# One load queue in order of use, split PSUM banks and quarter-width first matmuls in the opening of a grouped-query attention kernel

## Chip, cores, metric

The kernel runs on one core of one Trainium2 chip. The metric is the device time of one execution in microseconds (us). The time is 1.7 to 2 us longer than the span of the profile, which runs from the first to the last recorded event. All runs quoted here are fast (full granted clock), so they may be compared. "Faster" and "slower" mean by over 2%; the gain predicted here, 0.8 us, is about a tenth of that.

## The reference, cut to what matters

Two independent problems A and B of the same shapes; their outputs are concatenated.

```python
# x: 16 x 32 x 1024 (512 tokens of 1024), wq: 1024 x 4096, wo: 4096 x 1024, all bf16
# caches: 16 x 4 x 512 x 128; 32 query heads of 128 on 4 key heads
q = (x @ wq).reshape(B, Sq, 32, 128)            # projection, 32 heads
scores = q @ k.T * 128 ** -0.5                   # per head
o = softmax(scores) @ v
out = o.reshape(B, Sq, 4096) @ wo
```

## The kernel before

TensorE (PE) needs x transposed, with the 1024 features on the partitions. Four x tiles of 128 tokens (256 KB each; x0 to x3 below) are loaded into SBUF, the on-chip memory, and transposed on PE into PSUM, the memory in banks that PE writes to; VectorE (DVE) and ScalarE (ACT) copy the result back to SBUF. Then the first two heads are projected, in two halves of 256 tokens, while the rest is still loading. From head 2 on, a stream of matmuls of 512 columns keeps PE busy to the end. The change touches only what comes ahead of head 2. In the code, `warm_up(n)` does n matmuls on zeros that nobody reads, so that PE is busy before its data comes; the two between the transposes and the heads are called the filler below. In the profiles, PEld is PE's loading of weights, and SP (SyncE) and ACT each issue loads on a queue of their own.

```python
for j in range(2):                                   # loads: SP's queue and ACT's queue in turn
    for e, eng in enumerate((nc.sync, nc.scalar)):
        tt = 2 * j + e
        eng.dma_start(out=x_sb[:, tt, :], in_=x_v[:, tt, :])
    for e, eng in enumerate((nc.sync, nc.scalar)):   # heads 2j, 2j+1: lower and upper features
        cs, ns = slice(e * HC, (e + 1) * HC), slice(2 * j * DH, 2 * (j + 1) * DH)
        eng.dma_start(out=wq_tiles[0, 0][:, cs, ns], in_=wq_v[:, cs, ns])
load_wq(0, 1)                                        # 1 MB, SP; then keys, values, weights ...
# ... cut ...
def transpose_x(tt):
    xT_ps = psum.tile([P, DC, P], BF16, name="xT_ps", tag="s")
    for dc in range(DC):
        nc.tensor.transpose(xT_ps[:, dc, :], x_sb[:, tt, dc * P:(dc + 1) * P], ident[:])
    ts = slice(tt * P, (tt + 1) * P)
    nc.vector.tensor_copy(out=xT[0][:, 0:HC, ts], in_=xT_ps[:, 0:HC, :])
    nc.scalar.copy(out=xT[0][:, HC:DC, ts], in_=xT_ps[:, HC:DC, :])
# ... cut: first_heads(h, half) does 8 matmuls of 256 columns into head h's bank ...
warm_up(8)          # matmuls on zeros, nobody reads them
transpose_x(0)
transpose_x(1)
warm_up(2)
first_heads(0, 0)
transpose_x(2)
transpose_x(3)
first_heads(1, 0)
first_heads(0, 1)
first_heads(1, 1)
```

## Time and profile before

| | before |
|---|---|
| time at the prediction, median of 3 (range) | 350.65 us (350.25 to 350.69) |
| span of the profiled execution | 349.1 us (its time: 350.9 us) |
| PE busy | 340.7 us, 98% |
| first transpose starts | 4.90 us |
| head 2 starts / its copy starts | 11.54 / 13.70 us |

The page's busy times (busy us, share of the span, instructions) and the chain that ended last, by engine and by line:

```profile
PE 340.7 (98%) x2163; PEld 221.0 (63%) x2204; DVE 283.4 (81%) x421; ACT 179.6 (51%) x196; POOL 8.9 (3%) x21
...
PE 94%; DMA 3%; issue 1%; DVE 1%; ACT 0%; SPq 0%
```

PE bounds the kernel. The DMA share of the chain (11.7 us) lies wholly in the opening. The start of the same chain in order of time (start, us, what):

```profile
0.86 4.00 DMA x_sb<-in_A_x_dram
4.85 0.02 issue
4.87 7.71 DMA wq_sb<-in_A_wq_dram
12.58 0.05 issue
12.63 10.32 PE q_ps L312 x47
```

So the kernel waited for x tile 0 until 4.85, and then for a weight load that was issued at 4.87 and landed at 12.58. It is issued so late because it is the ninth load to be issued (the 1 MB load, written after it, goes ahead of it on SP's queue): the loads share eight semaphores, and the ninth waits until the first, x tile 0, has landed and its semaphore is free. The timeline of the opening (start, us of the whole group, engine, line, operation; in brackets the idle time of the engine ahead of it and what ended it):

```profile
4.90 1.24 PE L493 MATMUL xT_ps<-ident,x_sb 128*128 128x128 bf16 x16
5.73 0.87 DVE L497 COPY xT<-xT_ps 128x512 bf16<-128x512 bf16 x2 [3.28 <-PE xT_ps L493]
...
6.19 1.07 ACT L498 COPY xT<-xT_ps 128x512 bf16<-128x512 bf16 x2 [4.08 <-DVE xT L497]
...
6.66 1.26 PE L507 MATMUL q_ps<-xT,wq_sb 128*128 128x256 bf16 x8
...
7.92 1.07 PE L493 MATMUL xT_ps<-ident,x_sb 128*128 128x128 bf16 x16
...
8.82 2.81 PE L507 MATMUL q_ps<-xT,wq_sb 128*128 128x256 bf16 x24
...
11.54 11.40 PE L312 MATMUL q_ps<-xT,wq_sb 128*128 128x512 bf16 x50
...
13.70 0.58 ACT L320 CAST qT<-q_ps 128x512 bf16<-128x512 f32 x1 [3.59 <-PE q_ps L312]
...
15.43 0.58 ACT L320 CAST qT<-q_ps 128x512 bf16<-128x512 f32 x1 [1.14 <-PE q_ps L312]
```

Two things are to be read here. ACT's first copy was released by DVE's copy, not by PE: both read one PSUM bank, and DVE goes first. The Trainium skill, "PSUM — Partial Sum Buffer", section "PSUM bank collisions raise a hardware error", says that two engines may not access one bank and quadrant at once, reads included; the kernel's order agrees (DVE's first copy ends at about 6.16, ACT's starts at 6.19). And head 2's copy at 13.70 is a mark: the copies that follow it come every 1.73 us.

The windows view of the stretch in which four pieces of 256 KB landed (the last of x0 and x1 at 4.85, the last of the next four at 7.87; last columns: DMA share, that is the times of all packets over the time of 16 engines, which comes out above 1 here, and GB/s of all traffic):

```profile
core 0: us, PE busy (x) PEld busy (x) DVE busy (x) ACT busy (x) POOL busy (x), PEclk, DMA share, GB/s
4.85:7.87 3.02, 2.86 (x27) 1.95 (x26) 0.85 (x2) 1.07 (x2) 0.00 (x0) 1.00 1.11 344
```

### The profile page before, as it was taken

Reading aid. Unit: us, or ns where it says so; the run is one execution under the profiler, and the core shown is the slowest. Engines: PE = TensorE matmul, PEld = TensorE weight load, DVE = VectorE, ACT = ScalarE, POOL = GpSimd, SP = SyncE. Lnnn points to the kernel's source line nnn. Section 1 sums busy time; section 2 is a strip of 40 time slices with the busy share of each in tenths; the row PEclk is TensorE's granted clock in tenths of the full one; section 3 lists DMA queues with packets and bytes.
Section 4 is the critical chain, followed back from the end, with each engine's and each line's share of the span. In section 5 each row is a group of like instructions: output and inputs, shape, how many; then the busy total and the mean of one; then the engine's idle time right before and its main releaser. Section 6 shows DMA issues by size and latency. Waiting matters only on the chain.

```text
span 349.1 us, 5460 instructions
## 1 busy us (share of the span) xinstructions
PE 340.7 (98%) x2163; PEld 221.0 (63%) x2204; DVE 283.4 (81%) x421; ACT 179.6 (51%) x196; POOL 8.9 (3%) x21
## 2 busy tenths in 40 slices
PE   8999999999999999999999999999999999999995
PEld 4556666666666666666666666666666666666554
DVE  2218888988988898898889999999989999899710
ACT  2247667666666666666654454454454445445000
POOL 0000000000000000000000000000000000000010
PEclk9999999999999999999999999999999999999999
DMA  7999999999996999999999659996579975400000
GB/s 242 275 251 339 181 274 264 254 269 249 270 214 176 199 233 233 296 275 210 305 313 192 175 126 289 348 199 122 135 258 287 284 182 97 116 17 0 15 32 20
DMA packets 125085, 71.70 MB, mean 205 GB/s; under 512 B 73632, under 2 KB 124064, under 8 KB 125056
## 3 DMA queue, kind: packets, MB, share of 16 engines
q1 hardware_dynamic: 122848, 68.24, 81.1%
q0 software_dynamic: 720, 1.97, 1.6%
q10 hardware_dynamic: 1488, 1.11, 1.1%
q8 instruction: 18, 0.29, 0.4%
q14 instruction: 11, 0.09, 0.1%
HBM read 51.38 MB, written 2.10 MB: 153 GB/s over the span
## 4 chain that ended last, share of the span: by engine, by line
PE 94%; DMA 3%; issue 1%; DVE 1%; ACT 0%; SPq 0%
PE f_ps L331 31%; PE q_ps L312 30%; PE ob L431 16%; PE s_ps L371 16%; DMA wq_sb<-in_A_wq_dram 2%; DMA x_sb<-in_A_x_dram 1%; DVE parts L390 0%; PE sums L407 0%; DVE o_sb L343 0%; ACT o_sb L341 0%; DVE cs L399 0%; PE ok_ps L614 0%; SPq L651 0%
## 5 line engine op out<-in xcount | busy, mean ns | idle before, releaser
L379 ACT ACTIVATE p_sb<-s_ps,shift 128x1024 bf16<-128x1024 f32 x128 | 142.5, 1114 | 113.1 <-PE s_ps L371 100.4
L390 DVE TRANSPOSE_TENSOR_REDUCE parts<-p_sb 128x32 f32<-128x1024 bf16 x128 | 158.2, 1236 | 21.5 <-ACT p_sb L379 20.9
L331 PE MATMUL f_ps<-wo_sb,oT 128*128 128x512 bf16 (+1 forms) x524 | 127.9, 367 | 0.4
L312 PE MATMUL q_ps<-xT,wq_sb 128*128 128x512 bf16 x475 | 124.8, 380 | 0.6
L371 PE MATMUL s_ps<-qT,kT 128*128 128x256 bf16 x512 | 76.8, 273 | 0.9
L431 PE MATMUL ob<-p_sb,v_sb 128*128 128x256 bf16 x512 | 76.8, 273 | 0.6
L331 PEld LDWEIGHTS <-oT 128*128 128x128 bf16 x544 | 53.0, 98 | 33.8
L312 PEld LDWEIGHTS <-wq_sb 128*128 128x128 bf16 x496 | 48.3, 98 | 35.1 <-DMA wq_sb<-in_A_wq_dram 0.6
L371 PEld LDWEIGHTS <-kT 128*128 128x128 bf16 x512 | 56.9, 113 | 20.9
L431 PEld LDWEIGHTS <-v_sb 128*128 128x128 bf16 x512 | 50.1, 98 | 19.8 <-DVE oT L453 0.3
L453 DVE TENSOR_TENSOR oT<-r,ob 128x512 bf16<-128x512 f32 x64 | 43.9, 685 | 12.7 <-PE ob L431 9.3
L320 ACT CAST qT<-q_ps 128x512 bf16<-128x512 f32 x62 | 36.1, 583 | 23.7 <-PE q_ps L312 20.8
L418 DVE STREAM_TRANSPOSE r<-rall 128x512 f32<-128x512 f32 x64 | 45.5, 711 | 2.2
L407 PE MATMUL sums<-cs,fold 128*128 128x16 f32 x64 | 22.9, 357 | 0.1
L343 DVE CAST o_sb<-f_ps 128x512 bf16<-128x512 f32 (+1 forms) x16 | 10.8, 673 | 10.8 <-PE f_ps L331 10.0
L399 DVE TENSOR_REDUCE cs<-parts 128x16 fp32r<-128x64 f32 x64 | 16.9, 264 | 2.2
L407 PEld LDWEIGHTS sums<-cs,fold 128*128 128x128 f32 x64 | 12.1, 190 | 8.3 <-DVE cs L399 0.9
L345 POOL DMA_DIRECT2D out_dram<-o_sb x15 | 8.2, 549 | 329.7 <-DVE o_sb L343 299.0
L416 DVE RECIPROCAL rall<-sums 128x16 f32<-128x16 f32 x64 | 14.1, 220 | 0.0
L341 ACT CAST o_sb<-f_ps 128x256 bf16<-128x256 f32 x1 | 0.4, 372 | 22.1 <-PE f_ps L331 22.1
L497 DVE COPY xT<-xT_ps 128x512 bf16<-128x512 bf16 x4 | 1.7, 424 | 5.3 <-PE xT_ps L493 5.3
L484 PE MATMUL warm_ps<-warm 128*128 128x512 bf16 x10 | 4.2, 580 | 1.3 <-DVE warm L230 1.3
(26 smaller groups left out, 22.8 us busy)
## 6 DMA issues: line engine op xcount, KB each, us to landing
v_sb<-in_A_v_cache_dram SPq DMA_DIRECT2D x16, 512.0 KB, 4.9
wq_sb<-in_B_wq_dram SPq DMA_DIRECT2D x8, 1024.0 KB, 6.5
wo_sb<-in_A_wo_dram SPq DMA_DIRECT2D x8, 1024.0 KB, 7.6
v_sb<-in_B_v_cache_dram SPq DMA_DIRECT2D x16, 512.0 KB, 4.2
wo_sb<-in_B_wo_dram SPq DMA_DIRECT2D x8, 1024.0 KB, 9.2
wq_sb<-in_A_wq_dram SPq DMA_DIRECT2D x7, 1024.0 KB, 8.0
out_dram<-o_sb POOLq DMA_DIRECT2D x15, 128.0 KB, 3.1
kT<-in_A_k_cache_dram SPq DMA_TRANSPOSE x64, 4.5
```

The source lines that it names most:

```text
L312: nc.tensor.matmul(ps[:], lhsT=w[:, dc, (h % 4) * DH:(h % 4 + 1) * DH], rhs=xT[pr][:, dc, :], start=(dc == 0), stop=(dc == DC - 1),)
L320: nc.scalar.copy(out=qT[pr, g][:, :, hl, :], in_=ps[:].rearrange("p (b s) -> p b s", s=SQ),)
L331: nc.tensor.matmul(ps[:, 0:width], lhsT=oT[pr, tt][:, h, :], rhs=wo_tiles[pr, nh, h // REP][:, h % REP, off:off + width], start=(h == 0), ...
L371: nc.tensor.matmul(s_ps[:, c, :], lhsT=kT[:, i % GRP, c, :], rhs=qT[pr, g][:, b, :, :].rearrange("p h s -> p (h s)"), start=True, stop=True,)
L379: nc.scalar.activation(out=p_sb[:], in_=s_ps[:], func=ACTF.Exp, bias=shift[:], scale=SCALE)
L390: nc.vector.tensor_reduce(out=parts[j][:, q, :, :].rearrange("p c h -> p (c h)"), in_=st[i]["p"][:].rearrange("p c (h s) -> p (c h) s", s=SQ),
L399: nc.vector.tensor_reduce(out=cs[:], in_=parts.pop(j)[:].rearrange("p q c h -> p q h c"), axis=AX.X, op=ALU.add,)
L407: nc.tensor.matmul(sums[:], lhsT=fold[:].rearrange("p r s -> p (r s)"), rhs=cs[:].rearrange("p q h -> p (q h)"), start=True, stop=True,)
L416: nc.vector.reciprocal(out=rall[:, j, :], in_=pair.pop(j)[:])
L418: nc.vector.transpose(out=r[:].rearrange("p n s -> p (n s)"), in_=rall[:, j, :].unsqueeze(2).to_broadcast([P, 2 * REP, SQ]),)
L431: nc.tensor.matmul(ob[j][:, q, :], lhsT=v_sb[:, i % GRP, c, :], rhs=st[i]["p"][:, c, :], start=(c == 0), stop=(c == KC - 1),)
L453: nc.vector.tensor_tensor(out=out, in0=rcp.pop(j)[:].rearrange("p (q h) s -> p q h s", h=REP), in1=ob.pop(j)[:].rearrange("p q (h s) -> p ...
```

## The change

The intent: feed PE in the order in which it uses the data, from one queue, so that x tile 0 does not share the DMA engines with tile 1 and no early load is the ninth; give DVE and ACT separate PSUM banks, so that each copies as soon as its four transposes are done; do the second half of the tokens by quarters, so that work on tile 2 need not wait for tile 3; five warm-ups, not eight, as x comes sooner.

```diff
-            for j in range(2):
-                for e, eng in enumerate((nc.sync, nc.scalar)):
-                    ... (x tiles and first weights on SP's and ACT's queues in turn, as above)
+            # load_x and load_first_wq issue on nc.sync
+            load_x(0)
+            load_x(1)
+            load_first_wq(slice(0, 2 * DH), slice(0, HC))
+            load_first_wq(slice(0, 2 * DH), slice(HC, DC))
+            load_x(2)
+            load_x(3)
+            load_first_wq(slice(2 * DH, 4 * DH), slice(0, DC))
             load_wq(0, 1)
@@ transpose_x(tt)
-                xT_ps = psum.tile([P, DC, P], BF16, name="xT_ps", tag="s")
-                ... (eight transposes, then both copies)
+                bank = ("ob", "proj", "sums", "ob")[tt]
+                for cs, where_, copy in (
+                    (slice(0, HC), dict(tag="s"), nc.vector.tensor_copy),
+                    (slice(HC, DC), dict(tag=bank, bufs=2 if bank == "proj" else 1), nc.scalar.copy),
+                ):
+                    ... (four transposes, then this half's copy)
@@ order
-            warm_up(8)
+            warm_up(5)
             transpose_x(0)
             transpose_x(1)
             warm_up(2)
-            first_heads(0, 0)
+            for dcs in (lower, upper):
+                for h in range(2):
+                    first_heads(h, 0, 2, dcs)
             transpose_x(2)
             transpose_x(3)
-            first_heads(1, 0)
-            first_heads(0, 1)
-            first_heads(1, 1)
+            for h in range(2):
+                for tt in (2, 3):
+                    first_heads(h, tt, tt + 1, range(DC))
+            ... (head 0 cast by DVE, head 1 by ACT; before, both by DVE)
```

More of the change, by code (lines that the diff above doesn't have):

```diff
@@ L465, in fast_path, with load_x, load_first_wq @@
             HC = DC // 2
-            for j in range(2):
-                for e, eng in enumerate((nc.sync, nc.scalar)):
-                    tt = 2 * j + e
-                    eng.dma_start(out=x_sb[:, tt, :], in_=x_v[:, tt, :])
-                for e, eng in enumerate((nc.sync, nc.scalar)):
-                    cs, ns = slice(e * HC, (e + 1) * HC), slice(2 * j * DH, 2 * (j + 1) * DH)
-                    eng.dma_start(out=wq_tiles[0, 0][:, cs, ns], in_=wq_v[:, cs, ns])
+            def load_x(tt):
+                nc.sync.dma_start(out=x_sb[:, tt, :], in_=x_v[:, tt, :])
+            def load_first_wq(ns, cs):
+                nc.sync.dma_start(out=wq_tiles[0, 0][:, cs, ns], in_=wq_v[:, cs, ns])
+            load_x(0)
[5 more added lines that the diff above has]
+            load_first_wq(slice(2 * DH, 4 * DH), slice(0, DC))
             load_wq(0, 1)
@@ L490, in transpose_x, with first_heads @@
             def transpose_x(tt):
-                xT_ps = psum.tile([P, DC, P], BF16, name="xT_ps", tag="s")
-                for dc in range(DC):
-                    nc.tensor.transpose(
-                        xT_ps[:, dc, :], x_sb[:, tt, dc * P:(dc + 1) * P], ident[:]
-                    )
-                ts = slice(tt * P, (tt + 1) * P)
-                nc.vector.tensor_copy(out=xT[0][:, 0:HC, ts], in_=xT_ps[:, 0:HC, :])
-                nc.scalar.copy(out=xT[0][:, HC:DC, ts], in_=xT_ps[:, HC:DC, :])
-            first_q = [psum.tile([P, NW], FP32, name="q_ps", tag="proj") for _ in range(2)]
+                ts = slice(tt * P, (tt + 1) * P)
+                bank = ("ob", "proj", "sums", "ob")[tt]
[3 more added lines that the diff above has]
+                ):
+                    xT_ps = psum.tile([P, HC, P], BF16, name="xT_ps", **where_)
+                    for k, dc in enumerate(range(cs.start, cs.stop)):
+                        nc.tensor.transpose(
+                            xT_ps[:, k, :], x_sb[:, tt, dc * P:(dc + 1) * P], ident[:]
+                        )
+                    copy(out=xT[0][:, cs, ts], in_=xT_ps[:])
             qT[0, 0] = blk_tile([P, B, REP, SQ], "qT")
-            HN = NTOK // 2
-            def first_heads(h, half):
-                ts = slice(half * HN, (half + 1) * HN)
-                for dc in range(DC):
+            def first_heads(h, t0, t1, dcs):
+                ts = slice(t0 * P, t1 * P)
+                for dc in dcs:
                     nc.tensor.matmul(
@@ L513, in first_heads @@
                     )
-                if half == 1:
-                    nc.vector.tensor_copy(
-                        out=qT[0, 0][:, :, h, :],
-                        in_=first_q[h][:].rearrange("p (b s) -> p b s", s=SQ),
-                    )
-            warm_up(8)
+            lower, upper = range(HC), range(HC, DC)
+            warm_up(5)
             transpose_x(0)
             transpose_x(1)
+            first_q = [psum.tile([P, NW], FP32, name="q_ps", tag="proj") for _ in range(2)]
             warm_up(2)
-            first_heads(0, 0)
+            for dcs in (lower, upper):
+                for h in range(2):
+                    first_heads(h, 0, 2, dcs)
             transpose_x(2)
             transpose_x(3)
-            first_heads(1, 0)
-            first_heads(0, 1)
-            first_heads(1, 1)
+            for h in range(2):
+                for tt in (2, 3):
+                    first_heads(h, tt, tt + 1, range(DC))
+            for h, copy in enumerate((nc.vector.tensor_copy, nc.scalar.copy)):
+                copy(
+                    out=qT[0, 0][:, :, h, :],
+                    in_=first_q[h][:].rearrange("p (b s) -> p b s", s=SQ),
+                )
             def stream():
```

## The prediction

> **What bounds the kernel now.** TensorE. The table of busy time gives PE 340.7 of 349.1 us (98%), at full granted clock in all 40 slices; the chain that ended last is PE for 94% and DMA for 3%, all in the first 12.6 us: x tile landing at 4.85, weights of the first group landing at 12.58, then projection matmuls back to back. After that I find no PE wait for a load. So only the opening can be shortened, and a saving there should pass unchanged to the end.
>
> **The opening before (timeline, first 14 us).** Eight cold warm-up matmuls (0.427 us apart, from 1.29). First transpose at 4.89, when x tile 0 lands. PE reaches double rate (128 columns: 0.107 to 0.056 us) at 5.3. Transposes of tiles 0 and 1 end at 5.93; weights land at 6.45 (wait 0.42); 0.24 us at 7.3, because ScalarE's copy waits for VectorE's of the same bank; 0.29 us for tile 2; heads 0 and 1 end at 11.36; head 2 waits 0.18 us for the cast that frees its bank and 0.56 us for its upper weights. Those were the ninth load: ScalarE's queue issued it only at 4.87, when tile 0 had landed (a shared semaphore comes free), and it shared the DMA engines with a 1 MB load: 7.7 us to landing. Head 2's copy starts at 13.70; from there PE is periodic (1.726 us per head).
>
> **What the change does.**
> - One queue: data flow at about 340 GB/s from about 2.9 us, 0.77 us per 256 KB (estimate from the windows). Tile 0 no longer shares with tile 1. The Trainium skill, "DMA: Bandwidth & Descriptors", section "Queues, rings and completion order", says each engine takes turns between queue rows; the packet records agree (both queues move equal packets from 3.0 to 4.0). Estimated landings: x0 4.1 (was 4.85), x1 4.75, weights 5.5 and 6.3 (6.45, 5.87), x2 7.05, x3 7.8, second weights 9.4 (8.73 and 12.58). Only eight loads, so none waits for a semaphore. Issue costs 0.47 us each, faster than data.
> - Separate banks: VectorE copies (0.424 us) start after four transposes; ScalarE's (0.588) no longer wait for them.
> - Quarters: 32 matmuls of 128 columns at 0.056 = 1.8 us for 16 of 256 at 0.108 = 1.73: nearly free. Three warm-ups removed: off the path. One cast (0.69 us, DVE) becomes ACT (0.58).
>
> Estimated PE: transposes 4.1 to 5.6; warm-up to 6.05; first half of both heads (1.73) to 7.8; tiles 2 and 3 to 8.7; quarters with 0.3 us of waits for ScalarE's copies to 10.9; head 2 from 10.95 without a stop; its copy at 12.9, not 13.70. Saving 0.8 us: 350.65 - 0.8 = 349.85.
>
> **Predicted: 349.8 us, 349.2 to 350.9.** Faster by over 2%: 0.01; within 2%: 0.98; slower: 0.01.
>
> **What would show it.** First transpose near 4.1; no PE wait for DMA after 8 us; head 2's copy near 12.9; the same 1.726 us per head after; PE busy nearly equal; span about 0.8 us less.
>
> **What would make it wrong.** The clock. Five warm-ups end at 3.4, then PE idles 0.6 us until x0. The skill, "TensorE: Matmul & The Clock Gate", Part 1, says full rate comes after a busy window of about 3.4 us that runs freely; before, the step came 4.0 us after the first matmul, with no idle between. If the gap costs that window, the step moves to about 8.7: about 3 us lost, 352 to 353 us. I give this 15%. Or one queue starts slower than two, and x1 lands after 5.

## The result, and the profile after

Ratios are the mean time of one kernel's fast runs over that of the other's in the same rounds, so not quite the ratio of the medians.

| | before | after |
|---|---|---|
| time, median of 4 (range) | 350.54 us (350.25 to 350.69) | 350.36 us (350.13 to 350.43) |
| ratio to before, 95% interval | | 0.9995 (0.9977 to 1.0012): same |
| span of the traced execution | 349.1 | 348.6 |
| first transpose | 4.90 | 3.55 |
| head 2's copy starts | 13.70 | 13.26 |

The page's busy times and the chain by engine, after:

```profile
PE 342.2 (98%) x2217; PEld 221.2 (63%) x2217; DVE 282.6 (81%) x420; ACT 180.4 (52%) x197; POOL 8.9 (3%) x21
...
PE 96%; DMA 2%; SPq 1%; DVE 1%; issue 0%; ACT 0%
```

(The 1.5 us more of PE busy are not more work of that size: the trace of before lacks 41 matmul records. It has 2163 matmuls to 2204 weight loads, and, by line, 475 projection matmuls where after has 496.) The chain in order of time, after:

```profile
...
3.35 5.48 DMA x_sb<-in_A_x_dram
8.83 0.05 issue
8.88 0.62 PE xT_ps L506 x8
9.50 1.95 PE q_ps L516 x32
11.45 11.27 PE q_ps L312 x52
```

The late weight load has gone from the chain, and another load has taken its place: x tile 3, landing at 8.83. (That it was issued at 3.35, as the sixth on one queue, is not what made it late: the third, issued at 1.78, landed only at 5.71.) The timeline, after:

```profile
3.55 1.56 PE L506 MATMUL xT_ps<-ident,x_sb 128*128 128x128 bf16 x16
...
4.20 0.42 DVE L509 COPY xT<-xT_ps 128x512 bf16<-128x512 bf16 x1 [1.75 <-PE xT_ps L506]
...
4.62 1.11 ACT L509 COPY xT<-xT_ps 128x512 bf16<-128x512 bf16 x2 [2.51 <-PE xT_ps L506]
...
5.76 1.92 PE L516 MATMUL q_ps<-xT,wq_sb 128*128 128x256 bf16 x16 [0.21 <-DMA wq_sb<-in_A_wq_dram]
...
7.81 0.62 PE L506 MATMUL xT_ps<-ident,x_sb 128*128 128x128 bf16 x8
...
8.88 0.62 PE L506 MATMUL xT_ps<-ident,x_sb 128*128 128x128 bf16 x8 [0.45 <-DMA x_sb<-in_A_x_dram]
...
9.34 2.11 PE L516 MATMUL q_ps<-xT,wq_sb 128*128 128x128 bf16 x32
...
11.34 11.38 PE L312 MATMUL q_ps<-xT,wq_sb 128*128 128x512 bf16 x52
...
13.26 0.58 ACT L320 CAST qT<-q_ps 128x512 bf16<-128x512 f32 x1 [1.19 <-PE q_ps L312]
...
14.99 0.58 ACT L320 CAST qT<-q_ps 128x512 bf16<-128x512 f32 x1 [1.14 <-PE q_ps L312]
```

ACT is now released by PE, so the split banks do what they were meant to. x tile 0 is 1.35 us earlier. But tiles 2 and 3 come so late that PE's weight loads wait 0.41 and 0.62 us for them. The waits of the weight-load stage up to 23 us hold these two and the wait of 0.85 us for x tile 0 in one line (total us, times, longest):

```profile
PEld L506 <- DMA x_sb<-in_A_x_dram: 1.9, 3, 0.8
...
PEld L516 <- DMA wq_sb<-in_A_wq_dram: 0.7, 1, 0.7
```

The window from x1's landing to that of the fourth piece after it, after:

```profile
4.21:8.83 4.62, 3.88 (x38) 2.72 (x36) 1.26 (x3) 1.48 (x3) 0.00 (x0) 1.00 0.99 285
```

The same four pieces took 4.62 us, where before they took 3.02.

### The profile page after: what moved, and what is told of

Its sections match the earlier page's. It is cut to its first block, busy times and chain, and to the rows that moved or that the text cites. A ratio compares the mean times of both kernels' runs of the same rounds, so it can differ in the third digit from the quotient of the medians.

```text
span 348.6 us, 5527 instructions
## 1 busy us (share of the span) xinstructions
PE 342.2 (98%) x2217; PEld 221.2 (63%) x2217; DVE 282.6 (81%) x420; ACT 180.4 (52%) x197; POOL 8.9 (3%) x21
## 4 chain that ended last, share of the span: by engine, by line
PE 96%; DMA 2%; SPq 1%; DVE 1%; issue 0%; ACT 0%
PE f_ps L331 32%; PE q_ps L312 31%; PE ob L431 16%; PE s_ps L371 16%; DMA x_sb<-in_A_x_dram 2%; PE q_ps L516 1%; SPq L468 0%; DVE parts L390 0%; PE sums L407 0%; SPq L471 0%; DVE o_sb L343 0%; PE xT_ps L506 0%; ACT o_sb L341 0%; DVE cs L399 0%; PE ok_ps L627 0%
## 5 line engine op out<-in xcount | busy, mean ns | idle before, releaser
L331 PE MATMUL f_ps<-wo_sb,oT 128*128 128x512 bf16 (+1 forms) x544 | 133.3, 367 | 0.0
L312 PE MATMUL q_ps<-xT,wq_sb 128*128 128x512 bf16 x496 | 129.6, 380 | 0.0
L509 ACT COPY xT<-xT_ps 128x512 bf16<-128x512 bf16 x4 | 2.3, 585 | 5.7 <-PE xT_ps L506 5.7
```

The lines of the kernel that those rows point to most:

```text
L312: nc.tensor.matmul(ps[:], lhsT=w[:, dc, (h % 4) * DH:(h % 4 + 1) * DH], rhs=xT[pr][:, dc, :], start=(dc == 0), stop=(dc == DC - 1),)
L331: nc.tensor.matmul(ps[:, 0:width], lhsT=oT[pr, tt][:, h, :], rhs=wo_tiles[pr, nh, h // REP][:, h % REP, off:off + width], start=(h == 0), ...
```

## The experiments

The theories:

- **A**: one queue brings the opening loads more slowly than two did (1.15 us per 256 KB, not 0.77).
- **B**: the slow stretch was an accident of one execution.
- **C**: the five warm-ups let the step of the PE clock to full rate come late, and so gave the early x back.
- **D**: part of the gain read from the traces was never there, as the traced execution of before was a slow one.

Three marks are read in each trace. *Landings*: when the last of the 16 completion records of a load came. *Step*: when the trace's clock record goes to full rate; the spacing of matmuls of 128 columns falls there from 0.107 to 0.056 us. (The granted clock column of the windows view shows 1.00 on both sides of it.) *Copy*: the start of head 2's copy. From its start to the start of the last copy of an output tile took 331.11 to 331.13 us in all fourteen traces, so the copy holds everything that the opening did to the time of the traced execution. What follows, from the start of the last output copy until the span ends, varied from 3.80 to 4.29 us, which is more than half of the gain that is looked for.

Times below are medians, beside the kernel before in the same rounds.

| run | loads | warm-ups | x0 | x1 | last of next four | step | copy | time | before | ratio (95%) |
|---|---|---|---|---|---|---|---|---|---|---|
| before | two queues | 8 | 4.85 | 4.62 | 7.87 | 5.30 | 13.70 | 350.54 | | |
| after | one queue | 5 | 3.50 | 4.21 | 8.83 | 4.63 | 13.26 | 350.36 | 350.54 | 0.9995 (0.9977 to 1.0012) |
| after_again | one queue | 5 | 3.58 | 4.22 | 8.14 | 6.94 | 13.15 | 350.62 | 350.39 | 1.0007 (0.9993 to 1.002) |
| loads_only | one queue | 8 | 3.40 | 4.14 | 8.66 | 5.87 | 13.78 | 350.85 | 350.39 | 1.0014 (1.0 to 1.0028) |
| compute_only | two queues | 5 | 4.79 | 4.53 | 7.79 | 7.48 | 14.04 | 351.70 | 350.39 | 1.0038 (1.0025 to 1.0052) |
| two_queues | two queues | 5 | 4.77 | 4.50 | 7.75 | 9.19 | 14.86 | 352.02 | 350.39 | 1.0046 (1.0032 to 1.006) |
| after_warm8 | one queue | 8 | 3.61 | 4.30 | 8.81 | 4.63 | 13.24 | 350.94 | 350.62 | 1.0009 (0.9996 to 1.0022) |
| compute_only_warm8 | two queues | 8 | 4.88 | 4.66 | 7.93 | 5.95 | 13.64 | 350.50 | 350.62 | 0.9996 (0.9983 to 1.0008) |
| two_queues_warm8 | two queues | 8 | 4.91 | 4.69 | 7.93 | 6.98 | 13.85 | 350.67 | 350.62 | 0.9997 (0.9984 to 1.001) |
| x_first_warm8 | one queue | 8 | 3.54 | 4.17 | 9.01 | 5.92 | 13.69 | 351.04 | 350.62 | 1.0015 (1.0003 to 1.0028) |
| before_again | two queues | 8 | 4.83 | 4.56 | 7.81 | 5.15 | 13.57 | 350.76 | 350.74 | 1.0007 (0.9995 to 1.0019) |
| fewer_loads_warm8 | one queue, merged | 8 | 4.55 | 4.55 | 7.71 | 6.23 | 13.36 | 349.98 | 350.74 | 0.9983 (0.997 to 0.9996) |
| two_queues_no_filler | two queues | 8 | 4.81 | 4.60 | 7.83 | 4.23 | 13.08 | 350.31 | 350.74 | 0.9994 (0.9982 to 1.0007) |
| after_merged | one queue, partly merged | 5 | 3.59 | 4.36 | 8.90 | 5.44 | 13.97 | 350.80 | 350.68 | 1.0012 (0.999 to 1.0034) |

All outputs are right. The first four experiments ran together on one chip, the next four and then three on a second, the last on a third; across these groups only the ratios compare.

### after_again: the changed kernel, unaltered

> The changed kernel once more. Theory A (one queue feeds the opening more slowly): x0 lands near 3.5 us and x1 near 4.2 again, but the next four pieces of 256 KB take about 1.1 to 1.2 us each, not 0.77, so x3 lands near 8.8 and PE waits about 0.4 and 0.6 us for x2 and x3. Head 2's copy starts near 13.3, time 0.2 to 0.5 us under before. Rival B (the slow stretch was an accident of that one execution): x3 lands by 8.0 and head 2's copy starts near 12.9, time 0.8 us under before.

x0 and x1 landed as in the first trace, and the next four pieces took 3.92 us: slow again, if less so than 4.62. Theory A stands and B falls. The copy came at 13.15, 0.11 earlier than in the first trace although the step came 2.3 us later. The time was not under before's, as A expected, but 0.2 us over it; the interval leaves no room for the 0.8 us predicted.

### loads_only: the loads of after in the kernel before

```diff
 (before.py)
-   loads in turn on SP's and ACT's queues
+   the seven loads of after on SP's queue
```

> Before's compute with the new loads. Theory A: x3 again lands near 8.8 (before: 7.55), its transposes end near 9.4 and, as half of head 1 still stands behind them, head 2's copy starts near 14.1: 0.3 to 0.5 us slower than before. Rival B (the one queue delivers as I estimated, x3 at 7.8, second weights at 9.4): head 2's copy near 13.2, 0.4 us faster than before.

x3 landed at 8.66, the copy came at 13.78 and the time was 0.14% over before: the new loads alone gain nothing. The copy was later than before's 13.70 by 0.1 us, not by the 0.4 that A expected; the median, 0.46 us over before, is in its range.

### compute_only: the banks, order and quarters of after with the loads of before

```diff
 (after.py)
-   the seven loads of after on SP's queue
+   loads in turn on SP's and ACT's queues, as before
```

> The new banks, order, quarters and five warm-ups with before's loads in two queues. The upper half of the second weights is still the ninth load and lands near 12.6, so head 2 waits for it whatever the order ahead of it: head 2's copy at 13.6 to 13.7, no difference from before (within 0.2 us). If it is faster by 0.4 or more, the compute part carries the gain and that late load was not the limit.

This missed: it was 1.3 us slower. x0 lands at 4.79 with these loads, and the five warm-ups end at 3.6, so PE stands idle for 1.2 us; the step then came at 7.48, and the transposes of the first two tiles ran at half rate. This is the risk named in the prediction, in a kernel where the idle time is really there.

### two_queues: the loads of after in turn on two queues, without a ninth

```diff
 (after.py)
-   nc.sync.dma_start(out=x_sb[:, tt, :], in_=x_v[:, tt, :])
+   (nc.sync, nc.scalar)[tt % 2].dma_start(out=x_sb[:, tt, :], in_=x_v[:, tt, :])
-   load_first_wq(slice(0, 2 * DH), slice(HC, DC))
+   load_first_wq(slice(0, 2 * DH), slice(HC, DC), nc.scalar)
```

> The changed kernel with its seven first loads given in turn to two queues (x0, first lower weights, x2, second weights on one; x1, first upper weights, x3 on the other), so that no load is the ninth. Theory A: landings as before (x0 4.85, x2 7.9, x3 7.6), second weights by 10, PE waits at x0 and at the first weights (6.4) but not at x3; head 2's copy near 13.1, that is 0.6 us under before and 0.1 to 0.2 under the changed kernel. Rival B: no difference in rate between one queue and two; landings of all pieces then as in the changed kernel but x0 later, and head 2's copy at 13.4 or later.

The landings were those that A expected: x2 and x3 at 7.75 and 7.40, the second weights at 9.53. The time was not, for the cause of the run before: the step came at 9.19 and the run was the slowest of all. PE's part of the timeline, two_queues:

```profile
4.82 1.89 PE L506 MATMUL xT_ps<-ident,x_sb 128*128 128x128 bf16 x16 [1.22 <-DMA x_sb<-in_A_x_dram]
...
7.35 2.81 PE L516 MATMUL q_ps<-xT,wq_sb 128*128 128x256 bf16 x16
```

### after_warm8, compute_only_warm8, two_queues_warm8: eight warm-ups in the three kernels

```diff
-            warm_up(5)
+            warm_up(8)
```

> The changed kernel with eight warm-ups instead of five, so that PE has no idle time from 1.3 us until after x1 has landed. Theory C (what the change gained by the early x0 it gave back in the clock step, which moved between 4.6 and 6.9 us in its two traces, because the five warm-ups leave PE idle in the window that decides it): step by 5.9 at the latest as in before, head 2's copy near 13.0, runs closer together than 0.3 us, median 0.2 to 0.5 us under the changed kernel's. Rival A alone (only the slow single queue matters): no change, median 350.4 to 350.6, as PE waits for x2 and x3 anyway.

> Before's two queues and eight warm-ups with the new banks and order. Theory C: the 1.3 us that the five warm-ups cost with these loads (x0 at 4.8) come back whole: 350.3 to 350.5, equal to before, clock step at 5 to 6, head 2 waiting for its upper weights at 12.5. If it stays above 351, the new order itself costs time and not the clock.

> Two queues without a ninth load and with eight warm-ups. Theory A and C together: step at 5 to 6, no wait for x2 and x3, nor for the second weights; head 2's copy near 13.1, median 0.3 to 0.6 us under before. If the step alone was at fault in the run without the three warm-ups, that run's 352.0 falls by about 1.7 us.

In the two kernels with loads on two queues the three warm-ups were worth what C said: 351.70 became 350.50 and 352.02 became 350.67 (ratios 1.0038 to 0.9996, and 1.0046 to 0.9997); each taken against before of its own rounds, that is 1.4 and 1.6 us. PE's timeline, two_queues_warm8, the same two groups as above:

```profile
4.95 1.89 PE L506 MATMUL xT_ps<-ident,x_sb 128*128 128x128 bf16 x16
...
7.24 1.91 PE L516 MATMUL q_ps<-xT,wq_sb 128*128 128x256 bf16 x16
```

The 16 first matmuls took 1.91 us, not 2.81, as the step (6.98, there 9.19) now lay ahead of them. Still the copy came at 13.85, not 13.1: with the step at 6.98 the transposes and the two filler warm-ups ahead of the heads ran at half rate.

For the changed kernel itself C falls: with eight warm-ups it was no better (350.94 beside 350.62), and its copy at 13.24 was that of after. There x0 lands at 3.50, just as the fifth warm-up ends (3.61 by the trace, which models the ends of matmuls; the first transpose starts at 3.55), so there was no idle time to mend.

compute_only_warm8 equals before, as expected, and its chain says why:

```profile
4.91 7.62 DMA wq_sb<-in_A_wq_dram
12.52 0.05 issue
12.57 3.63 PE q_ps L312 x16
```

Whatever the banks and the order save, head 2 stands waiting for the ninth load. With the old loads the compute part of the change shows no gain.

### x_first_warm8: all x tiles ahead of the weights

```diff
 (after.py, eight warm-ups)
             load_x(1)
-            load_first_wq(lower)
-            load_first_wq(upper)
             load_x(2)
             load_x(3)
+            load_first_wq(lower)
+            load_first_wq(upper)
 transposes of all four tiles, then both heads in matmuls of 512 columns, no filler
```

> One queue, but all four x tiles first and then the first weights; both heads in matmuls of 512 columns. Theory A in the form that rows of 512 bytes are what one queue moves slowly: x0 to x3 land every 0.7 us (3.5, 4.2, 4.9, 5.6), the first weights at about 6.8 and 7.8. In the form that one queue is slow with any rows, x3 lands after 6.3. Head 2's copy 12.3 to 12.7 in the first form, median 0.7 to 1.1 us under before.

x2, a load of 2 KB rows like x0 and x1, landed at 6.46, 2.3 us after x1, and x3 at 7.28. So it is not the 512-byte rows of the weights that one queue moves slowly. The 16 completion records of x1 lie between 3.84 and 4.17; those of x2 between 4.59 and 6.46. Some of the 16 engines were about 1.9 us behind others from there on, and stayed so through the next four loads. The copy came at 13.69: the first weights landed at 8.13, not 6.8.

### before_again: the kernel before, for a second trace

> The kernel before, for a second trace. Theory D (half of the gain that I read from two traces was never there: the trace of before was of an execution of 350.9 us, the slowest of its first five): this trace's head 2 copy starts earlier than 13.70, near 13.2 if its span is the usual 348.5, and the upper half of its second weights lands before 12.3. Rival: head 2's copy at 13.6 to 13.8 with a span of 349.0 or more.

Its copy came at 13.57, between what D and its rival expected. But its span was 348.8 us, not the 348.5 for which D had named 13.2, so this trace alone does not settle D. The two traces of before have their copy at 13.70 and 13.57, the two of after at 13.26 and 13.15, 0.43 us earlier (means of two each). Their executions, however, took 350.9 and 350.74 us, and 350.43 and 350.42 us: 0.40 us apart (means; over different chips), where the medians of the same rounds have after 0.18 us under before, and after_again 0.23 us over it. The spans say the same. Beside after_again, nine executions of before had a median span of 348.5 us; less 331.12 and the 4.15 to 4.29 us at the end in the traces of before, that puts its usual copy at 13.1 to 13.2 (an estimate), where the trace of after_again has 13.15. So D holds for more than this one trace shows, and a gain of 0.43 us by the change is not shown.

### fewer_loads_warm8: three merged loads on the one queue

```diff
 (after.py, eight warm-ups)
-            load_x(0)
-            load_x(1)
-            load_first_wq(lower)
-            load_first_wq(upper)
-            load_x(2)
-            load_x(3)
+            load_x(slice(0, 2))
+            load_first_wq(both halves)
+            load_x(slice(2, 4))
```

> One queue, eight warm-ups, but the first six pieces merged into three of 512 KB (x0 with x1, both halves of the first weights, x2 with x3). If each further load on a queue brings its own gap, fewer loads land sooner: x2 and x3 by 8.0, time 0.3 us or more under the changed kernel with eight warm-ups. If one queue is slow whatever its loads, x3 lands at 8.5 to 9.0 as there, and the time is the same; x0 then comes later (4.3), behind the warm-ups.

x0 and x1 landed at 4.55, the first weights at 6.31, x2 and x3 at 7.71, the second weights at 9.49: the four pieces in 3.16 us, nearly as fast as two queues (2.98 to 3.05 in seven traces). The window of those pieces, fewer_loads_warm8:

```profile
4.55:7.71 3.16, 3.16 (x28) 2.79 (x28) 0.85 (x2) 1.17 (x2) 0.00 (x0) 1.00 1.10 346
```

So theory A in its plain form falls too. One queue is not slow in itself: it was in the five traces so far that start with two loads of 256 KB, and not in this one. This is the only version whose interval lies wholly below before (0.997 to 0.9996); its median is 0.76 us under before, where that of after_warm8 was 0.32 us over it, so the 0.3 us expected were exceeded. Its chain has no load in it:

```profile
1.29 3.59 PE warm_ps L488 x8
4.88 1.60 PE xT_ps L503 x16
6.48 0.43 PE warm_ps L488 x2
6.91 1.75 PE q_ps L513 x16
8.66 0.89 PE xT_ps L503 x16
9.55 1.99 PE q_ps L513 x32
```

One caution: its copy came at 13.36, only 0.21 us ahead of before_again and behind that of after_warm8 (13.24, in the fastest of that kernel's five executions). Another 0.28 us of its shorter span come from the end, from the last output copy on (3.87 us, where before_again had 4.15). So the time is shown, but how much of it is the opening is not. The two kernels with merged loads had the two shortest ends, 3.87 and 3.80; whether that belongs to the edit was not tested.

### two_queues_no_filler: two queues, eight warm-ups, no filler

```diff
 (two_queues_warm8)
             transpose_x(1)
-            warm_up(2)
```

> Two queues without a ninth load, eight warm-ups, and no warm-ups between the transposes and the first heads. In the trace of that kernel with them the step came at 6.98, so they ran at half rate, 0.85 us, and the first heads started at 7.24 though their weights had landed at 6.50. Without: first heads at 6.5 to 6.7, head 2's copy at 13.0 to 13.3 whatever the step, runs nearer together, median 0.2 to 0.5 us under before: the best version so far. If the step moves a window later (beyond 8.5), it is slower than before instead.

The first heads started at 6.46, the copy came at 13.08, the earliest of all traces. The step, however, came at 4.23 here, so this trace does not show what the filler costs when the step is late. The time was 350.31 beside 350.74; the interval holds 1, and the runs spread over 1 us (349.80 to 350.84), no nearer together than before.

### after_merged: the changed kernel with two merged loads

```diff
 (after.py)
             load_x(0)
             load_x(1)
-            load_first_wq(lower)
-            load_first_wq(upper)
-            load_x(2)
-            load_x(3)
+            load_first_wq(both halves)
+            load_x(slice(2, 4))
```

> The changed kernel with one edit: both halves of the first weights in one load, x2 and x3 in one load; x0 and x1 still alone, five warm-ups. If it is the number of small loads behind each other on one queue that starves it, x0 and x1 land at 3.5 and 4.2, the first weights at 5.9 to 6.1, x2 and x3 at 7.4 to 7.6, head 2's copy at 12.9 to 13.1: 0.6 us or more under before, as far below the changed kernel. If already the third load of a queue comes late whatever its size (1.2 to 2.3 us behind the second in the traces so far), the weights land at 6.5 or later and x3 after 8.0, and it is no better than the version with three merged loads (349.98 beside 350.74). Where the clock step comes late (after 7), up to 1 us is lost again in single runs, as the five warm-ups do not reach x0.

The second case: the weights landed at 7.31, their completion records spread from 5.79 to 7.31, x2 and x3 at 8.90; no gain. PE waited 1.38 us for the weights:

```profile
7.36 1.92 PE L514 MATMUL q_ps<-xT,wq_sb 128*128 128x256 bf16 x16 [1.38 <-DMA wq_sb<-in_A_wq_dram]
```

So merging the loads behind the first two does not help. In all six one-queue traces that begin with two loads of 256 KB, the third load on the queue came late: 1.2 to 2.3 us behind the second where it was 256 KB, 2.95 us where it was 512 KB (1.76 us for the same 512 KB in fewer_loads_warm8). Counted from the landing of the first 512 KB, the next 512 KB took 2.34 to 3.11 us in these six, 1.55 to 1.62 us from two queues, and 1.76 us in fewer_loads_warm8. In x_first_warm8 the third load had been issued by 2.2 us, and yet the DMA traffic fell after 3.75, as its windows show (last column):

```profile
3.00:3.75 0.75, 0.75 (x3) 0.28 (x2) 0.00 (x0) 0.00 (x0) 0.00 (x0) 1.00 1.08 363
3.75:4.50 0.75, 0.75 (x3) 0.30 (x2) 0.00 (x0) 0.00 (x0) 0.00 (x0) 1.00 0.65 169
4.50:5.25 0.75, 0.75 (x7) 0.57 (x6) 0.00 (x0) 0.00 (x0) 0.00 (x0) 1.00 1.02 311
```

The packet records tell the two kinds apart as well. Most packets of 2 KB took about 0.085 us and most of 512 bytes 0.027 us; of the loads' packets that began between 3.5 and 8 us, 10 to 24 took over 0.2 us (the longest 0.46 to 0.86 us) in each of the six slow traces, and none to two did in the other eight. So the slow stretch is made of single long packets, which put some engines behind, and of gaps. What causes them was not shown, and stays open.

## Why the prediction was right or wrong, point by point

The time, 350.36 us, fell in the range and in the class that had 0.98. That says little: the range, 349.2 to 350.9, holds before's own 350.65 too, so a change that gains nothing would have fallen in it as well. The point, 349.8, was 0.56 us too low, and the saving of 0.8 us that it stands for did not show in the timings.

- **"Only the opening can be shortened, and a saving there should pass unchanged to the end"**: right. From head 2's copy to the last output copy all fourteen traces agree within 0.02 us.
- **"Tile 0 no longer shares with tile 1", x0 at 4.1, x1 at 4.75**: right in direction, too cautious in size: 3.50 and 4.21. The turn-taking between queue rows, which the prediction takes from the Trainium skill, "DMA: Bandwidth & Descriptors", section "Queues, rings and completion order", agrees with the traces: from two queues the tiles landed within 0.3 us of each other (4.62 and 4.85), from one 0.7 us apart.
- **"0.77 us per 256 KB"**, landings "x2 7.05, x3 7.8, second weights 9.4": this is the term that was mis-sized. It was read from traces of two queues and given to one. Measured 1.15 us per piece (4.62 / 4): x2 7.76, x3 8.83, second weights 10.62. "No PE wait for DMA after 8 us" was wrong with it: PE waited for x3 at 8.83.
- **"Only eight loads, so none waits for a semaphore"**: right; the wait for the ninth load is gone, and it was the last load on the chain before (and in compute_only_warm8).
- **"Separate banks", "Quarters ... nearly free"**: right. ACT is released by PE; the 32 quarter matmuls started at 9.34 and head 2 at 11.34, 0.2 us over 32 times 0.056. With the old loads they show no gain, which the prediction did not say.
- **"Head 2 from 10.95, its copy at 12.9"**: measured 11.34 and 13.26. Of the 0.8 us predicted, the traces show 0.44 in the first pair and 0.42 in the second, and those are traces of slower executions of before and faster ones of after (see before_again).
- **The timings show less still**: 0.9995 and 1.0007, where 0.43 us would be 0.9988. The first interval holds that, the second does not. No gain by the change is shown in the time. How much of the missing 0.8 us the slow loads account for is shown only in part: in the trace of after, x3 landed 1.03 us and the copy started 0.36 us later than predicted. The step, which varied from execution to execution, is a likely part of the rest, and was not tested for it.
- **"Five warm-ups end at 3.4, then PE idles 0.6 us"**: wrong for this kernel, as x0 came at 3.50. The mechanism was right: with x0 at 4.8 the same five warm-ups cost 1.4 and 1.6 us (compute_only, two_queues, and their twins with eight). The loss was smaller than the prediction's about 3 us for a step at 8.7, as the steps at 7.48 and 9.19 show. The Trainium skill, "TensorE: Matmul & The Clock Gate", Part 1, says that the window runs freely and that the step varies from run to run. The traces agree: in nine traces with eight warm-ups the step came between 4.23 and 6.98, in the two with five and x0 at 4.8 at 7.48 and 9.19.

## What to carry to other kernels

When loads move from two queues to one, do not keep the rate that was read from two: check the landing of the third load, not of the first, and try a larger first load (512 KB here, in one trace) or two queues. Where PE waits for its first data, cover the wait with warm-up matmuls to its end, and count them anew whenever the data's arrival moves. For a gain of a tenth of a per cent, a mark at the end of the changed stretch tells where time went in one execution; but a kernel's executions differ by as much, so compare the time of each traced execution with its kernel's median before two traces are subtracted.

## What the Trainium skill lacked or had wrong

- "DMA: Bandwidth & Descriptors", sections "Issuing engines are not separate DMA queues" and "Rules for kernel authors", say that issuing from several engines saves only the sequencer's issue time and does not help bandwidth. Here the same four pieces of 256 KB took 2.98 to 3.05 us from two queues (seven traces) and 3.92 to 4.84 us from one (five traces), with the issues on each queue about 0.5 us apart in both, and all six pieces issued by 3.8 us. So the saved issue time is not the difference. Merged into loads of 512 KB, one queue did it in 3.16 us. The page's advice to coalesce agrees with that.
- No page tells of a late third load behind two loads of 256 KB on a queue, with engines drifting apart: completion records of one load spread over 0.33 us for the second and 1.87 us for the third (x_first_warm8).
- "TensorE: Matmul & The Clock Gate", Part 1, asks for a busy window of about 3.4 us. In one trace the step came 2.94 us after the first matmul (4.23 and 1.29, two_queues_no_filler), and over the nine traces with eight warm-ups between 2.9 and 5.7 us after it.
- No page says what three warm-ups fewer, and so 1.2 us of idle time ahead of the first work, do to the step; here it came at 7.48 and 9.19 (one trace each), and the time rose by 1.4 and 1.6 us.
